# Searching the top 32 in maxima of four keys, with three pools of candidates, and turning 97 units on VectorE

## The chip, the cores and the metric

The kernel runs on one core of a Trainium2 chip. The metric is the device time of one execution, in microseconds; smaller is better. The trace was taken by the hardware profiler on one execution, and names of lines (L483) are lines of the kernel before. Engines are TensorE (PE in the profile; PEld is its weight load), VectorE (DVE), ScalarE (ACT), GpSimd (POOL) and the queue of SyncE (SP), from which nearly all transfers are issued.

## What is computed

Attention that keeps, for each query, the 32 largest of 576 scores, followed by a normalization, a two-layer network and a residual:

```python
scores = scale * np.matmul(q, k.transpose(0, 1, 3, 2))      # (8, 8, 576, 576), head size 64
kth = np.partition(scores, -32, axis=-1)[..., -32:-31]
scores = np.where(scores >= kth, scores, -1e9)
scores = scores - np.max(scores, axis=-1, keepdims=True)
attn = np.exp(scores)
attn = attn / (np.sum(attn, axis=-1, keepdims=True) + 1e-09)
x = heads_joined(np.matmul(attn, v))                        # (8, 576, 512)
xn = (x - mean(x)) / np.sqrt(var(x) + 1e-06) * g_ln
out = x + np.maximum(xn @ w_ch1, 0.0) @ w_ch2               # 512 -> 2048 -> 512
```

All numbers are 32-bit floats. The two weight matrices arrive as 64-bit floats and are converted in the kernel.

## The kernel before

The work is cut into 160 units. A full unit (128 of them) is one block of 128 queries of two heads: two tiles of 128 x 576 scores. A rest unit (32) holds the last 64 queries of two heads in one tile. Units stand in jobs: a job is one batch entry, one pair of heads and one, two or three query blocks. The order of the jobs is written out by hand, and the whole order of instructions too: the loop `for n in range(END)` (L1263) runs one step per unit, and in each step every engine gets pieces of work for several units. Every engine runs its instructions strictly in that order.

In step n the loop does this for VectorE's main thread: `select(u, 0)` to `select(u, 3)` for unit n, spread over the step, and at its end `halve` for unit n + 1. `halve` (L447) forms two arrays of 288 from the 576 scores of a tile: the larger and the smaller of the keys j and j + 288. `select(u, i)` (L464) is one of four search rounds: MAX8 gives the eight largest of a row, and, but for the last round, MATCH_REPLACE8 (preceded by a MATCH_VALUE_LOAD) overwrites these eight. Rounds 0 and 1 search the 288 larger keys; in round 1 the eight largest of the 288 smaller keys are taken as candidates as well, and rounds 2 and 3 search the larger keys and these candidates together (296). The eighth value of round 3 is the threshold. One step later ScalarE and GpSimd make the mask (`prepare`, `mask`), and ScalarE the exponentials (`weigh`, L543).

Eight candidates from the smaller keys are enough unless eight or more of a row's 32 largest lie there. `watch` (L498, GpSimd) writes for each tile the difference of the eighth candidate and the threshold; `settle_watch` (L509) reduces these notes once per 16 units, `tell` (L517) turns them into one flag at the end, and where the flag is set, the whole computation runs a second time with two rounds of candidates. `hi_homes` (L110) are the two buffers in which the larger keys and the candidates of a unit lie, used in turn; the candidates lie in front of the keys or behind them in turn, so that GpSimd can still read those of one unit while VectorE fills the buffer for the unit after next.

The exponentials then have to be turned (queries and keys exchanged) to become the moving operand of the product with v. There are two ways. `turn` (L597): TensorE transposes each full unit in nine pieces (four per tile, L606, and one for the last 64 keys of both, L635), and ScalarE copies them to the tile pt. `move` (L573): VectorE transposes blocks of 32 x 32 in one instruction (L577), SP writes the result to HBM and, one step later, reads it back in four pieces in the turned order into pt (L587). Which full unit takes which way is set at L1106, `u.moved`: 87 full units are moved. The product (`values`, L664) of a job stands four steps after the job's last unit where the next job's first unit is moved, three otherwise; a moved unit n is transposed in step n + 2 and its reads are issued in step n + 3. pt is a single buffer.

The network works on blocks of 256 rows (`Block`). Its matrix products (L819 hidden layer, L979 and L858 projection) are put in a list and handed out between the pieces of the attention. Up to the step in which the weights are converted (step 21), the share handed out per step follows from cost numbers of the planner (`DVE_UNIT` and others, `slot`); after it, the work in the list is spread evenly up to the next block and the end.

Of the kernel before, what the change touches and what calls it, by code (L numbers as in the profile page):

```python
# [10 lines left out]
ALU = mybir.AluOpType  # L11
FP32 = mybir.dt.float32
# [17 lines left out]
def compute(  # L30
# [12 lines left out]
    nc = tc.nc  # L43
    P = nc.NUM_PARTITIONS
    B, H, S, D = q.shape
# [11 lines left out]
    def pool(name, bufs, **kw):  # L57
        return ctx.enter_context(tc.tile_pool(name=name, bufs=bufs, **kw))

    NV = 2  # L60
    GQ = 2 * P + R
    HALF = S // 2
    LOWS = 8 * low_rounds

    consts = pool("consts", 1)
    ldpool = pool("ld", 1)
# [3 lines left out]
    lopool = pool("lo", 1)  # L70
# [20 lines left out]
    def const(shape, name):  # L91
        return consts.tile(shape, FP32, tag=name, name=name)

    def brief(name):

        return psps.tile([P, 512], FP32, tag="ps", name=name)
# [8 lines left out]
    ends = const([P, P], "ends")  # L105
    nc.gpsimd.memset(ends[:], 0.0)
    if doubt is not None:
        watched = const([P, 2, 34], "watched")
        nc.gpsimd.memset(watched[:], -1.0)
    hi_homes = [const([P, 2, HALF + (1 if doubt is None else 2) * LOWS], f"hi{i}") for i in range(2)]  # L110
    ident = const([P, P], "ident")
    make_identity(nc, ident[:])
    columns = const([P, J + NC], "columns")
    half, gcol = columns[:, 0:J], columns[:, J : J + NC]
# [300 lines left out]
    def take_scores(u):  # L415
        u.sc = scpool.tile([P, 2, S], FP32, tag="sc", name="sc")
        for t in range(len(u.tiles)):
            for s in range(2):
                nc.scalar.copy(  # L419
                    u.sc[:, t, s * HALF : (s + 1) * HALF], u.made[s][t][:, 0:HALF]  # L420
                )

    def score_half(u, s):
# [5 lines left out]
        for ps, hs in zip(pss, u.tiles):  # L429
            for i, hh in enumerate(hs):  # L430
                r = slice(hh * D, (hh + 1) * D)
                parts = [(0, s * HALF, HALF)]
                if u.rest and hh == 1:
                    parts = [(0, R + s * HALF, HALF - s * R)]
                    if s:
                        parts += [(HALF - R, 0, R)]
                for o, k0, width in parts:
# [9 lines left out]
    def halve(u):  # L447

        nt = len(u.tiles)
        u.lo = lopool.tile([P, 2, HALF], FP32, tag="lo", name="lo")
        u.hi = hi_homes[u.i % 2]
        sides = int(doubt is not None)
        u.low, u.body = (sides * LOWS + HALF, sides * LOWS) if doubt is None or u.i // 2 % 2 else (0, LOWS)
        a, b = u.sc[:, 0:nt, 0:HALF], u.sc[:, 0:nt, HALF:S]
        lo, hi = u.lo[:, 0:nt], u.hi[:, 0:nt, u.body : u.body + HALF]  # L460
        nc.vector.tensor_tensor(hi, a, b, ALU.max)  # L461
        nc.vector.tensor_tensor(lo, a, b, ALU.min)  # L462

    def select(u, i):  # L464

        nt = range(len(u.tiles))

        def replace(m, t, x):
            nc.vector.match_replace(x, m[:, t, :], x, LOWEST)  # L469

        if i == 1:
            for r in range(low_rounds):
                o = u.low + 8 * r
                for t in nt:
                    nc.vector.max(u.hi[:, t, o : o + 8], u.lo[:, t])  # L475
                if r < low_rounds - 1:
                    for t in nt:
                        replace(u.hi[:, :, o : o + 8], t, u.lo[:, t])
        r0, width = (min(u.low, u.body), HALF + LOWS) if i > 1 else (u.body, HALF)
        pl = brief_small if i in (1, 2) else small  # L480
        m = pl.tile([P, 2, 8], FP32, tag=f"m{i}", name=f"m{i}")
        for t in nt:
            nc.vector.max(m[:, t, :], u.hi[:, t, r0 : r0 + width])  # L483
        if i < TOP_K // 8 - 1:
            for t in nt:
                replace(m, t, u.hi[:, t, r0 : r0 + width])
        if i == 0:
            u.top = m
        u.thr = m
# [8 lines left out]
    def watch(u):  # L498

        nt = len(u.tiles)  # L500
        half, c = u.i // 16 % 2, 1 + 2 * (u.i % 16)
        nc.gpsimd.tensor_tensor(
            watched[:, half, c : c + nt], u.hi[:, 0:nt, u.low + 7], u.thr[:, 0:nt, 7], ALU.subtract
        )
        if u.i % 16 == 15 or u.i == N - 1:
            u.ends_watch = True
            u.half = half

    def settle_watch(half):  # L509

        for out, first, op in ((0, 0, ALU.max), (33, 1, ALU.min)):
            nc.vector.tensor_reduce(
                watched[:, half, out : out + 1], watched[:, half, first : first + 33],
                mybir.AxisListType.X, op,
            )

    def tell():  # L517

        w = hpool.tile([P, J * P], FP32, tag="h", name="tell")
        nc.gpsimd.memset(w[:], 0.0)  # L520
        nc.vector.tensor_scalar(w[:, 2:4], watched[:, :, 33], -1.0e38, None, ALU.is_le)
        nc.vector.tensor_scalar(w[:, 4:6], watched[:, :, 0], 0.0, None, ALU.is_ge)
        nc.vector.tensor_reduce(w[:, 0:1], w[:, 2:6], mybir.AxisListType.X, ALU.max)
        ps = brief("tell")
        nc.tensor.transpose(ps[:, 0:P], w[:, 0:P], ident[:])
        nc.vector.tensor_reduce(w[0:1, P : P + 1], ps[0:1, 0:P], mybir.AxisListType.X, ALU.max)
        nc.vector.tensor_copy(doubt, w[0:1, P : P + 1])
# [560 lines left out]
    N = len(units)  # L1088
# [15 lines left out]
    for j, nj in zip(jobs, jobs[1:] + [None]):  # L1104
        for u in units[max(j.first, EARLY) : j.last + 1]:
            u.moved = not u.rest and u.i >= jobs[3 * NHP].first and (  # L1106
                u.i < j.last
                or (j.b > 1 and (j.hp % 2 == 0 or u.i > N - 20))
                and nj is not None and not units[nj.first].rest
            )  # L1110

# [16 lines left out]
    for j in jobs:  # L1128
        if j.hp == NHP - 1:
            b = j.b  # L1130
# [26 lines left out]
    def at(i):  # L1157
        return units[i] if 0 <= i < N else None
# [96 lines left out]
    take_scores(units[0])  # L1255
    load(fresh[1], nc.sync, nc.scalar)
    halve(units[0])
    scores(units[1])
    take_scores(units[1])
# [3 lines left out]
    for n in range(END):  # L1263
# [8 lines left out]
        u, nxt, mk = at(n), at(n + 1), at(n - 1)  # L1272
# [21 lines left out]
        if mk and doubt is not None:  # L1294
            watch(mk)
# [12 lines left out]
        if u:  # L1308
            select(u, 0)
# [15 lines left out]
        if doubt is not None and at(n - 2) and at(n - 2).ends_watch:  # L1325
            settle_watch(at(n - 2).half)
            if n == N + 1:
                tell()
# [12 lines left out]
        if u:  # L1341
            select(u, 1)
# [33 lines left out]
        if u:  # L1376
            select(u, 2)
# [19 lines left out]
        if nxt:  # L1397
            halve(nxt)
# [14 lines left out]
        if late and late.job.hp == NHP - 1:  # L1413
            r = late.job.b // 2
# [14 lines left out]
@with_exitstack  # L1429
def kernel(  # L1430
    ctx: ExitStack,
    tc: tile.TileContext,
    *operands: bass.AP,
):
    nc = tc.nc
    doubt = ctx.enter_context(tc.tile_pool(name="doubt", bufs=1)).tile(
        [1, 1], I32, tag="doubt", name="doubt"
    )
    compute(tc, *operands, low_rounds=1, doubt=doubt[:])
    again = nc.values_load(  # L1440
        doubt[:], min_val=0, max_val=1,
        skip_runtime_bounds_check_because="a comparison's result",
    )
    with tc.If(again > 0):
        compute(tc, *operands, low_rounds=2, doubt=None)
# [31 lines left out]
```

## Time and profile before

| | |
|---|---|
| median of 3 runs | 1571.16 us (1571.02 to 1571.75) |
| profiled execution | 1571.11 us, of which the span of the trace is 1569.2 us |
| TensorE busy | 1469.0 us (94%) |
| VectorE busy | 1363.4 us (87%) |
| ScalarE busy | 1083.8 us (69%) |
| GpSimd busy | 981.2 us (63%) |
| mean granted clock of TensorE | 0.975 |
| bytes moved | 245.60 MB, 157 GB/s |

Busy time is the time in which an engine executes something, not counting waits, branches and the issuing of transfers. In the profile's groups, `out<-in` are the kernel's names of tiles, then follow the shape, the count, the total and the mean duration of one, and the idle time of the engine just before them. In a view of windows, each stretch of the span shows the busy time of each engine with its number of instructions, the granted clock, the share of time in which the DMA engines were busy, and GB/s. In the timeline, the first number is the start and the second the time until the end of the last instruction of the row. The duration of an instruction on VectorE or TensorE reaches into that of the next; the distance between starts tells what one costs when they follow each other.

### The profile page before, as it was taken

Reading aid. Unit: us, or ns where it says so; the run is one execution under the profiler, and the core shown is the slowest. Engines: PE = TensorE matmul, PEld = TensorE weight load, DVE = VectorE, ACT = ScalarE, POOL = GpSimd, SP = SyncE. Lnnn points to the kernel's source line nnn. Section 1 sums busy time; section 2 is a strip of 40 time slices with the busy share of each in tenths; the row PEclk is TensorE's granted clock in tenths of the full one; section 3 lists DMA queues with packets and bytes.
Section 4 is the critical chain, followed back from the end, with each engine's and each line's share of the span. In section 5 each row is a group of like instructions: output and inputs, shape, how many; then the busy total and the mean of one; then the engine's idle time right before and its main releaser. Section 6 shows DMA issues by size and latency. Waiting matters only on the chain. (4 is left out here: it accounts for less than half of the span.)

```text
span 1569.2 us, 27215 instructions
## 1 busy us (share of the span) xinstructions
PE 1469.0 (94%) x8046; PEld 1108.0 (71%) x8046; DVE 1363.4 (87%) x3873; ACT 1083.8 (69%) x3081; POOL 981.2 (63%) x1318
## 2 busy tenths in 40 slices
PE   4568889999999999999999999999999998999997
PEld 3346446566787677778777777777777776788886
DVE  7997999899979998999988999999999999768000
ACT  6978887786777767767768676768676776555421
POOL 6968995747465565756566647474746475737524
PEclk9779989999999999999999999999999999999999
DMA  6623551466728865577754687657677557454511
GB/s 170 167 85 97 137 139 53 124 178 181 226 83 194 202 208 153 168 199 153 216 148 134 174 200 197 173 150 191 175 201 206 162 164 208 121 166 125 150 35 50
DMA packets 374774, 245.60 MB, mean 157 GB/s; under 512 B 255956, under 2 KB 343512, under 8 KB 374616
## 3 DMA queue, kind: packets, MB, share of 16 engines
q1 hardware_dynamic: 371048, 243.17, 57.6%
q8 instruction: 67, 1.10, 0.3%
q10 hardware_dynamic: 3568, 0.59, 0.3%
q14 instruction: 91, 0.75, 0.2%
HBM read 166.14 MB, written 77.53 MB: 155 GB/s over the span
## 5 line engine op out<-in xcount | busy, mean ns | idle before, releaser
L535 POOL TENSOR_TENSOR e<-e,sc 128x576 f32<-128x576 f32 x288 | 416.0, 1462 | 453.8 <-ACT e L532 392.9
L819 PE MATMUL hps<-xT,w 128*128 128x256 f32 x2304 | 542.2, 384 | 2.4 <-ACT xT L781 2.4
L819 PEld LDWEIGHTS hps<-xT,w 128*128 128x128 f32 x2304 | 423.0, 191 | 82.2 <-issue 27.2
L483 DVE MAX8 m<-hi 128x8 f32<-128x296 f32 (+1 forms) x1152 | 471.3, 444 | 1.2
L469 DVE MATCH_REPLACE8 hi<-m,hi 128x288 f32<-128x288 f32 (+1 forms) x864 | 377.0, 441 | 0.0
L979 PE MATMUL ops<-w,h 128*128 128x256 f32 x1280 | 304.8, 383 | 1.4 <-ACT o L944 1.4
L979 PEld LDWEIGHTS ops<-w,h 128*128 128x128 f32 x1280 | 233.6, 190 | 44.3 <-issue 13.5
L419 ACT COPY sc<-scps 128x288 f32<-128x288 f32 x576 | 188.5, 402 | 78.5 <-POOL e L535 56.2
L543 ACT ACTIVATE e<-e,m 128x576 f32<-128x576 f32 x288 | 225.1, 784 | 14.6 <-POOL e L535 12.5
L532 ACT ACTIVATE e<-sc,m 128x576 f32<-128x576 f32 x288 | 209.4, 769 | 0.0
L842 ACT ACTIVATE h<-hps 128x512 f32<-128x512 f32 x144 | 86.7, 602 | 114.1 <-PE hps L819 113.5
L577 DVE STREAM_TRANSPOSE sc<-e 128x1152 f32<-128x1152 f32 x87 | 118.8, 1366 | 52.5 <-ACT e L543 46.3
L669 PE MATMUL av<-pt,vb 128*64 128x256 f32 (+2 forms) x1280 | 148.8, 376 | 9.5 <-DMA pt<-turned 7.7
L462 DVE TENSOR_TENSOR lo<-sc 128x576 f32<-128x576 f32 (+1 forms) x160 | 136.1, 850 | 0.0
L461 DVE TENSOR_TENSOR hi<-sc 128x576 f32<-128x576 f32 (+1 forms) x160 | 130.0, 812 | 3.0 <-ACT sc L419 3.0
L669 PEld LDWEIGHTS av<-pt,vb 128*64 128x64 f32 x1280 | 81.6, 140 | 66.4 <-issue 17.1
L438 PE MATMUL scps<-kT,late_qT 64*128 64x288 f32 (+3 forms) x832 | 121.7, 410 | 0.2 <-ACT pt L618 0.2
L979 PE MATMUL ops<-wt,s 128*128 128x256 f32 x512 | 119.4, 383 | 0.0
L475 DVE MAX8 hi<-lo 128x8 f32<-128x288 f32 x288 | 117.5, 443 | 0.0
L438 PE MATMUL scps<-kT,qT 64*128 64x288 f32 x512 | 92.6, 460 | 23.5 <-DVE qT L366 8.0
L606 PE MATMUL tp<-ident,e 128*128 128x128 f32 x456 | 74.2, 290 | 39.9 <-ACT e L543 28.9
L979 PEld LDWEIGHTS ops<-wt,s 128*128 128x128 f32 x512 | 94.7, 190 | 17.3 <-issue 4.4
(111 smaller groups left out, 1793.5 us busy)
## 6 DMA issues: line engine op xcount, KB each, us to landing
turned<-sc SPq DMA_DIRECT2D x87, 576.0 KB, 4.2
pt<-turned SPq DMA_DIRECT2D x348, 144.0 KB, 3.2
w<-forms SPq DMA_DIRECT2D x128, 256.0 KB, 4.7
vb<-in_v_dram SPq DMA_DIRECT2D x80, 288.0 KB, 4.2
raw<-in_moe_w_ch_dram SPq DMA_DIRECT2D x32, 512.0 KB, 4.5
kT<-kept SPq DMA_DIRECT2D x48, 288.0 KB, 3.7
kept<-kT SPq DMA_DIRECT2D x32, 288.0 KB, 3.6
kqin<-in_k_dram SPq DMA_DIRECT2D x116, 72.0 KB, 2.6
```

The costliest lines, as they stand in the source:

```text
L419: nc.scalar.copy(u.sc[:, t, s * HALF : (s + 1) * HALF], u.made[s][t][:, 0:HALF])
L438: nc.tensor.matmul(ps[i * R : i * R + ql, o : o + width], qT[r, q0 : q0 + ql], kT[r, k0 : k0 + width], start=True, stop=True,)
L461: nc.vector.tensor_tensor(hi, a, b, ALU.max)
L462: nc.vector.tensor_tensor(lo, a, b, ALU.min)
L469: nc.vector.match_replace(x, m[:, t, :], x, LOWEST)
L483: nc.vector.max(m[:, t, :], u.hi[:, t, r0 : r0 + width])
L532: nc.scalar.activation(u.e[:, t], u.sc[:, t], AF.Relu, bias=u.edge[:, t : t + 1], scale=-STEEP)
L535: nc.gpsimd.tensor_tensor(u.e[:, t], u.e[:, t], u.sc[:, t], ALU.subtract)
L543: nc.scalar.activation(u.e[:, t], u.e[:, t], AF.Exp, bias=u.bias[:, t : t + 1], scale=-scale, accum_out=g.den[:, col : col + 1],)
L669: nc.tensor.matmul(av[h * D : (h + 1) * D, 0 : g.nq], vb[:, h * (J + 1) + c, :], heads_of(g, h, 0, g.nq // 32)[:, :, c], start=(c == 0), s ...
L819: nc.tensor.matmul(ps[0][:, side * N : (side + 1) * N], w1[:, c, f * P : (f + 1) * P], self.xT[:, c, 0:N], start=(c == 0), stop=(c == NC - 1),
L979: nc.tensor.matmul(bank[name][:, 0:Q], a(j), rhs, start=first and j == 0, stop=(j == G - 1), skip_group_check=not first,)
```

## The change

The larger keys are halved a second time, into 144 maxima of four keys each (`hi`) and 144 smaller ones of the pairs' maxima (`mid`). Round 0 searches the 144 maxima alone. Three pools give eight candidates each: the two halves of `mid` (72 each, taken at the end of round 0) and the 288 smaller keys (taken in round 1, as before). Rounds 1 to 3 search the 144 maxima and the 24 candidates together, 168 elements. `watch` compares the eighth candidate of each of the three pools. The second computation, which runs only when the flag is set, keeps the old form. The rule for moved units now also takes the last unit of a job with an odd pair of heads where the batch entry is above 1, and that of an even pair where it is not; 97 full units are moved.

```diff
--- before.py
+++ after.py
@@ -59,8 +59,10 @@
 
     NV = 2
     GQ = 2 * P + R
-    HALF = S // 2
+    HALF, QUART = S // 2, S // 4
     LOWS = 8 * low_rounds
+    POOLS = 3
+    CANDS = 8 * POOLS
 
     consts = pool("consts", 1)
     ldpool = pool("ld", 1)
@@ -105,9 +107,11 @@
     ends = const([P, P], "ends")
     nc.gpsimd.memset(ends[:], 0.0)
     if doubt is not None:
-        watched = const([P, 2, 34], "watched")
+        NOTES = POOLS * 32
+        watched = const([P, 2, NOTES + 2], "watched")
         nc.gpsimd.memset(watched[:], -1.0)
-    hi_homes = [const([P, 2, HALF + (1 if doubt is None else 2) * LOWS], f"hi{i}") for i in range(2)]
+    home = HALF + LOWS if doubt is None else QUART + 2 * CANDS
+    hi_homes = [const([P, 2, home], f"hi{i}") for i in range(2)]
     ident = const([P, P], "ident")
     make_identity(nc, ident[:])
     columns = const([P, J + NC], "columns")
@@ -452,14 +456,25 @@
 
 
         nt = len(u.tiles)
+        u.hi = hi_homes[u.i % 2]
+        a, b = u.sc[:, 0:nt, 0:HALF], u.sc[:, 0:nt, HALF:S]
+        tt = nc.vector.tensor_tensor
+        if doubt is None:
+            u.lo = lopool.tile([P, 2, HALF], FP32, tag="lo", name="lo")
+            u.low, u.body, u.width = HALF, 0, HALF
+            tt(u.hi[:, 0:nt, 0:HALF], a, b, ALU.max)
+            tt(u.lo[:, 0:nt], a, b, ALU.min)
+            return
+        u.low, u.body = (CANDS + QUART, CANDS) if u.i // 2 % 2 else (0, CANDS)
+        u.width = QUART
+        pairs = lopool.tile([P, 2, HALF], FP32, tag="lo", name="pairs")
+        tt(pairs[:, 0:nt], a, b, ALU.max)
+        x, y = pairs[:, 0:nt, 0:QUART], pairs[:, 0:nt, QUART:HALF]
+        u.mid = lopool.tile([P, 2, QUART], FP32, tag="mid", name="mid")
+        tt(u.hi[:, 0:nt, u.body : u.body + QUART], x, y, ALU.max)
+        tt(u.mid[:, 0:nt], x, y, ALU.min)
         u.lo = lopool.tile([P, 2, HALF], FP32, tag="lo", name="lo")
-        u.hi = hi_homes[u.i % 2]
-        sides = int(doubt is not None)
-        u.low, u.body = (sides * LOWS + HALF, sides * LOWS) if doubt is None or u.i // 2 % 2 else (0, LOWS)
-        a, b = u.sc[:, 0:nt, 0:HALF], u.sc[:, 0:nt, HALF:S]
-        lo, hi = u.lo[:, 0:nt], u.hi[:, 0:nt, u.body : u.body + HALF]
-        nc.vector.tensor_tensor(hi, a, b, ALU.max)
-        nc.vector.tensor_tensor(lo, a, b, ALU.min)
+        tt(u.lo[:, 0:nt], a, b, ALU.min)
 
     def select(u, i):
 
@@ -468,15 +483,24 @@
         def replace(m, t, x):
             nc.vector.match_replace(x, m[:, t, :], x, LOWEST)
 
-        if i == 1:
-            for r in range(low_rounds):
-                o = u.low + 8 * r
+        if doubt is None:
+            if i == 1:
+                for r in range(low_rounds):
+                    o = u.low + 8 * r
+                    for t in nt:
+                        nc.vector.max(u.hi[:, t, o : o + 8], u.lo[:, t])
+                    if r < low_rounds - 1:
+                        for t in nt:
+                            replace(u.hi[:, :, o : o + 8], t, u.lo[:, t])
+            with_all, cands = i > 1, LOWS
+        else:
+            if i == 1:
                 for t in nt:
-                    nc.vector.max(u.hi[:, t, o : o + 8], u.lo[:, t])
-                if r < low_rounds - 1:
-                    for t in nt:
-                        replace(u.hi[:, :, o : o + 8], t, u.lo[:, t])
-        r0, width = (min(u.low, u.body), HALF + LOWS) if i > 1 else (u.body, HALF)
+                    nc.vector.max(u.hi[:, t, u.low : u.low + 8], u.lo[:, t])
+            with_all, cands = i > 0, CANDS
+        r0, width = u.body, u.width
+        if with_all:
+            r0, width = min(u.low, u.body), width + cands
         pl = brief_small if i in (1, 2) else small
         m = pl.tile([P, 2, 8], FP32, tag=f"m{i}", name=f"m{i}")
         for t in nt:
@@ -484,6 +508,14 @@
         if i < TOP_K // 8 - 1:
             for t in nt:
                 replace(m, t, u.hi[:, t, r0 : r0 + width])
+        if i == 0 and doubt is not None:
+            part = QUART // (POOLS - 1)
+            for t in nt:
+                for r in range(POOLS - 1):
+                    o = u.low + 8 + 8 * r
+                    nc.vector.max(
+                        u.hi[:, t, o : o + 8], u.mid[:, t, r * part : (r + 1) * part]
+                    )
         if i == 0:
             u.top = m
         u.thr = m
@@ -498,9 +530,13 @@
     def watch(u):
 
         nt = len(u.tiles)
-        half, c = u.i // 16 % 2, 1 + 2 * (u.i % 16)
+        half, c = u.i // 16 % 2, 1 + 2 * POOLS * (u.i % 16)
+        cands = u.hi[:, 0:nt, u.low : u.low + CANDS].rearrange("p t (r k) -> p t r k", k=8)
         nc.gpsimd.tensor_tensor(
-            watched[:, half, c : c + nt], u.hi[:, 0:nt, u.low + 7], u.thr[:, 0:nt, 7], ALU.subtract
+            watched[:, half, c : c + POOLS * nt].rearrange("p (t r) -> p t r", r=POOLS),
+            cands[:, :, :, 7],
+            u.thr[:, 0:nt, 7].unsqueeze(2).to_broadcast([P, nt, POOLS]),
+            ALU.subtract,
         )
         if u.i % 16 == 15 or u.i == N - 1:
             u.ends_watch = True
@@ -508,9 +544,9 @@
 
     def settle_watch(half):
 
-        for out, first, op in ((0, 0, ALU.max), (33, 1, ALU.min)):
+        for out, first, op in ((0, 0, ALU.max), (NOTES + 1, 1, ALU.min)):
             nc.vector.tensor_reduce(
-                watched[:, half, out : out + 1], watched[:, half, first : first + 33],
+                watched[:, half, out : out + 1], watched[:, half, first : first + NOTES + 1],
                 mybir.AxisListType.X, op,
             )
 
@@ -518,7 +554,7 @@
 
         w = hpool.tile([P, J * P], FP32, tag="h", name="tell")
         nc.gpsimd.memset(w[:], 0.0)
-        nc.vector.tensor_scalar(w[:, 2:4], watched[:, :, 33], -1.0e38, None, ALU.is_le)
+        nc.vector.tensor_scalar(w[:, 2:4], watched[:, :, NOTES + 1], -1.0e38, None, ALU.is_le)
         nc.vector.tensor_scalar(w[:, 4:6], watched[:, :, 0], 0.0, None, ALU.is_ge)
         nc.vector.tensor_reduce(w[:, 0:1], w[:, 2:6], mybir.AxisListType.X, ALU.max)
         ps = brief("tell")
@@ -1105,7 +1141,7 @@
         for u in units[max(j.first, EARLY) : j.last + 1]:
             u.moved = not u.rest and u.i >= jobs[3 * NHP].first and (
                 u.i < j.last
-                or (j.b > 1 and (j.hp % 2 == 0 or u.i > N - 20))
+                or (j.b > 1 or j.hp % 2 == 0)
                 and nj is not None and not units[nj.first].rest
             )
```

## Prediction

> **What bounds the kernel now.** I read the page's totals and slices first, then the busy time of each engine by stage, then what TensorE waited for in the long middle stage, then single rows for prices.
>
> ```profile
> span 1569.2 us, 27215 instructions
> PE 1469.0 (94%) x8046; PEld 1108.0 (71%) x8046; DVE 1363.4 (87%) x3873; ACT 1083.8 (69%) x3081; POOL 981.2 (63%) x1318
> ...
> PE   4568889999999999999999999999999998999997
> DVE  7997999899979998999988999999999999768000
> ```
>
> TensorE is full from about the seventh slice on; VectorE is nearly full too, and has stopped three slices before the end. The stages in the view of windows (PE, PEld, DVE, ACT, POOL busy, then the granted clock):
>
> ```profile
> 0.00:157.00 157.00, 101.49 (x500) 72.14 (x500) 131.86 (x370) 125.67 (x327) 121.11 (x120) 0.85 0.48 130
> 157.00:196.00 39.00, 32.12 (x146) 17.27 (x145) 38.82 (x91) 34.56 (x88) 36.19 (x32) 0.93 0.51 137
> 157.00:275.00 118.00, 103.78 (x483) 62.32 (x482) 117.58 (x316) 98.03 (x254) 96.27 (x88) 0.93 0.41 109
> 275.00:1450.00 1175.00, 1154.60 (x6528) 880.62 (x6530) 1108.30 (x3176) 829.11 (x2428) 712.88 (x1021) 1.00 0.64 173
> 1450.00:1569.00 119.00, 109.17 (x542) 92.95 (x538) 5.67 (x15) 30.98 (x74) 50.94 (x91) 0.97 0.28 77
> ```
>
> Of TensorE's 100 us of idle time (1569.2 - 1469.0), 70 lie before 275 us: 55.5 before 157 us and 14.2 from 157 to 275 us, where VectorE is busy 117.58 of 118 us and sets the pace. From 275 to 1450 us TensorE is idle 20.4 of 1175 us. Busy could hide slow running, so the spacing of its instructions matters:
>
> ```profile
> 803.52 0.60 PE L606 MATMUL tp<-ident,e 128*128 128x128 f32 x4
> 803.96 1.46 PE L979 MATMUL ops<-w,h 128*128 128x256 f32 x6
> 805.26 0.38 PE L714 MATMUL xo<-ident,oT 128*128 128x128 f32 x2
> ```
>
> Six 256-column products start in 1.30 us, 0.217 us each, and four transposes of 128 columns in 0.44 us, 0.11 us each: in proportion to their columns. So the queue runs at its rate, and from 275 us the time is TensorE's work plus 20 us of waits. The tail, in which VectorE has 5.67 us of work, is TensorE's alone. Hence work taken off VectorE counts only before 275 us, and work taken off TensorE counts where it is full.
>
> **Ten more units turned by VectorE.** The added units are 25, 29, 35, 47, 51, 55, 67, 79, 103 and 107, the last of their jobs. Each drops two parts of four transposes and one of the ends, 9 x 0.11 = 0.99 us; ten give **-9.9 us**, all where TensorE is full. ScalarE loses their 30 copies, which are not the bound. What they add:
>
> ```profile
> L577 DVE STREAM_TRANSPOSE sc<-e 128x1152 f32<-128x1152 f32 x87 | 118.8, 1366 | 52.5 <-ACT e L543 46.3
> ...
> turned<-sc SPq DMA_DIRECT2D x87, 576.0 KB, 4.2
> pt<-turned SPq DMA_DIRECT2D x348, 144.0 KB, 3.2
> ```
>
> VectorE gets 10 x 1.37 = 13.7 us, between about 270 and 970 us; cover is its idle time of 1175 - 1108.3 = 66.7 us in the middle stage together with what the search below frees. The transpose can wait for ScalarE's exponential; the third and fourth search rounds, the next halving and any column statistics queue behind it, and the next mask and ScalarE's bias wait for those. SP gets ten writes and forty reads: each read waits on SP for its write, and loads of keys, values, forms and stores stand behind it. The result is due one step after the read is issued, since the last unit of a job has the shortest time to its product:
>
> ```profile
> PE av L669 <- DMA pt<-turned: 7.7, 6, 2.9
> PE tp L778 <- ACT sc L419: 3.6, 3, 1.9
> PE tp L606 <- ACT sc L419: 3.0, 2, 1.6
> ```
>
> These are TensorE's longest waits between 275 and 1450 us (total, times, longest). Before, 19 moved units are last of their job, after, 29. If the 7.7 us belong to those 19, ten more cost 7.7 x 10/19 = **+4.1 us**; the bounds are 0 (all hidden) and 10 x 2.9 = 29 us (each as the longest). The other 12.7 us of waits hang on ScalarE's queue, which loses work; I take a quarter, **-3.2 us**, between 0 and -12.7.
>
> **The narrower search.** VectorE's cost is the distance between starts, not the printed duration, which overlaps the next one:
>
> ```profile
> 189.35 0.80 DVE L483 MAX8 m<-hi 128x8 f32<-128x288 f32 x2
> 190.07 0.07 DVE L469 MATCH_VALUE_LOAD hi<-m,hi 128x8 f32 x1
> ...
> 191.00 0.74 DVE L366 STREAM_TRANSPOSE kT<-kqin 128x576 f32<-128x576 f32 x1
> 191.67 0.40 DVE L366 STREAM_TRANSPOSE qT<-kqin 128x256 f32<-128x256 f32 x1
> 192.00 0.46 DVE L366 STREAM_TRANSPOSE late_qT<-kqin 128x320 f32<-128x320 f32 x1
> ...
> 195.53 0.74 DVE L462 TENSOR_TENSOR lo<-sc 128x576 f32<-128x576 f32 x1
> 196.20 0.81 DVE L483 MAX8 m<-hi 128x8 f32<-128x288 f32 x2
> ```
>
> The transposes give 0.67 us at 576 elements and 0.33 at 256: a line of 0.06 us plus 1.06 ns an element. It gives 0.365 at 288, and the MAX8 pair took 0.36 each; a TENSOR_TENSOR of 576 with nothing beside it took 0.67. By the line, 72, 144 and 168 elements cost 0.135, 0.21 and 0.235 us. Per full unit of two tiles:
> - MAX8: six of 288 and four of 296 (0.37), 3.64 us, become two of 144, four of 72, two of 288 and six of 168, 3.09 us: -0.55.
> - MATCH_REPLACE8, priced as MAX8 of its width: four of 288 and two of 296, 2.18 us, become two of 144 and four of 168, 1.36 us: -0.82. The six value loads stay.
> - TENSOR_TENSOR: two of 576, 1.34 us, become two of 576 and two of 288, 2.07 us: +0.73. The second reads what the first has just written; I add 0.1 us for it, the difference of duration and start distance (0.74 - 0.67) rounded up.
>
> That is -0.54 us. No row shows MAX8 narrower than 288: the far ends are a price in proportion to width, 0.09 at 72 elements, and a floor of 0.33, the narrowest pass quoted. I take the line, since the transposes lie on it.
>
> Against it stands what TENSOR_TENSOR costs beside GpSimd:
>
> ```profile
> 158.08 1.42 DVE L461 TENSOR_TENSOR hi<-sc 128x576 f32<-128x576 f32 x1
> 159.43 1.84 DVE L462 TENSOR_TENSOR lo<-sc 128x576 f32<-128x576 f32 x1
> 161.19 0.81 DVE L483 MAX8 m<-hi 128x8 f32<-128x288 f32 x2
> ```
>
> ```profile
> 158.85 1.79 POOL L183 TENSOR_TENSOR wt<-wt 128x512 uint32<-128x512 uint32 x1
> 160.72 1.68 POOL L185 TENSOR_TENSOR w<-wt,sign 128x512 f32<-128x512 f32 x1
> 162.38 1.18 POOL L165 TENSOR_SCALAR wt<-wt 128x512 f32<-128x512 f32 x2
> 163.53 3.13 POOL L535 TENSOR_TENSOR e<-e,sc 128x576 f32<-128x576 f32 x2
> 166.61 0.20 POOL L502 TENSOR_TENSOR watched<-hi,m 128x2 f32<-128x2 f32 x1
> 166.76 1.28 POOL L183 TENSOR_TENSOR wt<-wt 128x512 uint32<-128x512 uint32 x1
> ```
>
> The same instruction took 1.76 us between starts at 159.43 and 0.67 at 195.53; GpSimd's L183 took 1.79 there and 1.28 alone. The MAX8 rows keep their 0.36 us under GpSimd's work. So the change trades work that does not collide for work that does. The average collision by stage, from line 462's busy time:
>
> ```profile
> 0.00:157.00 157.00, 16.64 (x14) 0.85 0.48 130
> 157.00:275.00 118.00, 13.44 (x12) 0.93 0.41 109
> ```
>
> ```profile
> L462 DVE TENSOR_TENSOR lo<-sc 128x576 f32<-128x576 f32 x77 | 63.9, 830 | 0.0
> ```
>
> Before 275 us the mean is 30.08/26 = 1.157 us, 0.42 above the clean 0.74; from 400 to 1300 us it is 0.09 above. One more set of 576 elements therefore takes +0.42 early and +0.09 later: a full unit gains 0.12 us early and 0.45 later. Early, 26 units give **-3.1 us**; the bounds are -0.54 x 26 = -14 (no new collision) and, with the extra elements at the price of the row at 159.43, (1.76 - 0.67 - 0.54) x 26 = +14. Later the gain, some 0.45 x 102 = 46 us of VectorE's time, lies under TensorE and is worth nothing; without TensorE's full queue it would be.
>
> GpSimd is slowed as well. From 157 to 196 us it has 2.8 us left in some 3.5 steps, 0.8 a step; the collision of 1.79 - 1.28 = 0.5 us fits in. The wider watch writes 6 numbers instead of 2 at about 0.2 us and the two reductions per sixteen units read 97 instead of 33: nothing on the path, under GpSimd's and VectorE's slack of the middle stage; bare, 64 x 1.06 ns x 20 = 1.4 us.
>
> The Trainium skill (SBUF — State Buffer, "Who interferes with whom") says that a VectorE instruction with two SBUF inputs contends with a GpSimd one that reads SBUF, one with a single input does not, and that the loser is held for the whole instruction. The trace agrees on who collides; a full hold for every extra instruction gives the +14 us end instead of -3.1, so 1576 instead of 1559.
>
> **Sum.** -9.9 + 4.1 - 3.2 - 3.1 = -12.1. The profiled execution took 1571.11 us, 1.9 more than its span, and the median is 1571.16, so nothing is added: **1559 us**.
>
> **The rivals.**
> - A. The forecast: 1551 to 1567. Chance 0.60.
> - B. Early collisions do not grow and TensorE's waits close: 1571.1 - 9.9 - 14 - 6 = 1541. For it, VectorE is the pace-setter at 157 to 275 us; against it, GpSimd is nearly full there too. 0.16.
> - C. The collision on the shared port, before 275 us: every extra pass meets GpSimd, 1571.1 - 9.9 + 14 + 1 = 1576, slower. It decides once an early unit grows by more than (9.9 + 3.1)/26 = 0.50 us, near the row at 159.43. Against it, the mean of 26 units is far below that row. 0.09. The rule of the page named above is this case.
> - D. Width saves nothing below 256 elements: MAX8 then costs 0.36 x 2 + 0.33 x 12 = 4.68 (+1.04), MATCH_REPLACE8 1.98 (-0.20), with +0.83 for the passes and +0.42 for collisions +2.1 us a unit early, 1571.1 - 9.9 + 54 = 1615. Against it, the line. 0.02.
> - E. The ten new results land late: ten waits of 1.3 us (7.7/6), with the first gains: 1568; each as the longest, 1584. For it, the only long wait in the middle stage is this one. 0.12.
> - F. The change does not do what it says: a pool overflows and the whole is computed again, over 3100 us. In the reference's inputs, no row has more than 6 of its 32 largest in one of the three pools, and 8 are needed. 0.01.
>
> **How the numbers follow.** About 0.2% (3.1 us) is what a measurement can tell. Faster: A without its upper edge (0.59), B and a third of E, 0.79; same: that edge and half of E, 0.07; slower: C, D, F and the rest of E, 0.14. The range leaves out C and the far part of B: **1545 to 1570**.
>
> **What would show it.** VectorE's transposes 97 times; TensorE's transposes of e on its own queue 9 x 10 fewer and its busy time near 1459 us; MAX8 of 72 elements started 0.13 to 0.15 us apart, VectorE's busy time down by some 35 us (3 + 46 saved on full units, 14 added); the 26th halving 3 us earlier; waits of av for pt near 12 us. It is wrong if VectorE's TENSOR_TENSOR of 576 before 275 us averages over 1.5 us, if TensorE's idle time between 275 us and VectorE's end grows past 30 us, or if VectorE's end no longer lies before TensorE's tail.

## The result, and the profile after

The changed kernel takes 1648.13 us (median of 4 runs, 1647.36 to 1650.82) against 1571.09 us for the kernel before: a ratio of 1.0492, 95% interval 1.0474 to 1.0511. The change makes it 77 us slower; 1559 us had been predicted. The second computation did not run, and the intended instructions are there: 97 transposes by VectorE, MAX8 over 72 and 168 elements. The page of the profile after, totals and slices:

```profile
span 1645.8 us, 27978 instructions
PE 1485.9 (90%) x7956; PEld 1114.6 (68%) x7956; DVE 1459.2 (89%) x4779; ACT 1072.9 (65%) x3051; POOL 1038.0 (63%) x1318
...
PE   4678889989899889999999998899999898999997
DVE  7998999999989998999999999999999999977100
```

VectorE's busy time was to fall by some 35 us; it rose by 96 us (from 1363.4). The windows of the kernel after (columns as before):

```profile
0.00:157.00 157.00, 102.84 (x499) 73.03 (x500) 140.73 (x442) 125.65 (x326) 119.26 (x120) 0.84 0.48 129
157.00:275.00 118.00, 101.65 (x458) 61.16 (x458) 117.09 (x382) 96.25 (x251) 96.69 (x86) 0.93 0.42 111
275.00:1450.00 1175.00, 1095.70 (x6072) 824.67 (x6069) 1135.72 (x3753) 779.45 (x2292) 725.12 (x959) 0.98 0.64 173
```

In the middle stage TensorE is idle 79 us (1175 - 1095.7) instead of 20, and has done 6072 products instead of 6528. Nearly all of the loss is made there: before 275 us the two kernels differ little (the 26th halving starts 2.6 us later, at 271.1 instead of 268.5 us). Where VectorE's own stage ends is told by the first and last start of the halving's first pass, before and after:

```profile
L461 DVE TENSOR_TENSOR hi<-sc x160: 429/737/1978, 11.3 to 1440.8; 128x576 f32<-128x576 f32 x128, 128x288 f32<-128x288 f32 x32
```

```profile
L471 DVE TENSOR_TENSOR pairs<-sc x160: 429/739/1976, 11.2 to 1516.8; 128x576 f32<-128x576 f32 x128, 128x288 f32<-128x288 f32 x32
```

The last halving starts 76 us later, and what follows it takes the same in both: 1569.2 - 1440.8 = 128 us and 1645.8 - 1516.8 = 129 us. So the whole loss lies between the first and the last halving. VectorE's groups by shape name the place:

```profile
L477 DVE TENSOR_TENSOR lo<-sc 128x576 f32<-128x576 f32 x128 | 179.9, 1405 | 4.4
...
L471 DVE TENSOR_TENSOR pairs<-sc 128x576 f32<-128x576 f32 x128 | 118.5, 926 | 3.0 <-ACT sc L423 3.0
...
L474 DVE TENSOR_TENSOR hi<-pairs 128x288 f32<-128x288 f32 x128 | 88.4, 691 | 4.4
L475 DVE TENSOR_TENSOR mid<-pairs 128x288 f32<-128x288 f32 x128 | 83.0, 649 | 0.0
```

The pass for lo is the same instruction as L462 before, which took 918 ns on average:

```profile
L462 DVE TENSOR_TENSOR lo<-sc 128x576 f32<-128x576 f32 x128 | 117.6, 918 | 0.0
```

It now takes 1405 ns. The mean hides two values: 69 of the 128 took over 1.5 us, against 14 of 128 before, and 64 of these 69 begin while a mask subtraction of GpSimd (L571) is running. A step of the timeline shows why; first VectorE, then GpSimd, after:

```profile
995.25 0.74 DVE L471 TENSOR_TENSOR pairs<-sc 128x576 f32<-128x576 f32 x1
996.02 0.46 DVE L474 TENSOR_TENSOR hi<-pairs 128x288 f32<-128x288 f32 x1
996.39 0.45 DVE L475 TENSOR_TENSOR mid<-pairs 128x288 f32<-128x288 f32 x1
996.88 1.85 DVE L477 TENSOR_TENSOR lo<-sc 128x576 f32<-128x576 f32 x1
998.65 0.51 DVE L507 MAX8 m<-hi 128x8 f32<-128x144 f32 x2
```

```profile
996.46 3.54 POOL L571 TENSOR_TENSOR e<-e,sc 128x576 f32<-128x576 f32 x2 [1.68 <-ACT e L568]
```

And the same place in the kernel before:

```profile
973.69 0.74 DVE L461 TENSOR_TENSOR hi<-sc 128x576 f32<-128x576 f32 x1
974.35 0.75 DVE L462 TENSOR_TENSOR lo<-sc 128x576 f32<-128x576 f32 x1
975.01 0.81 DVE L483 MAX8 m<-hi 128x8 f32<-128x288 f32 x2
```

```profile
974.89 2.84 POOL L535 TENSOR_TENSOR e<-e,sc 128x576 f32<-128x576 f32 x2 [3.47 <-ACT e L532]
```

GpSimd's mask subtraction starts 1.2 us after the halving does, in both (996.46 - 995.25 and 974.89 - 973.69). It hangs on the threshold of the round that ends where the halving begins; between the two, ScalarE forms the bias and the first part of the mask:

```profile
995.36 0.21 ACT L527 ACTIVATE m<-m 128x2 f32<-128x2 f32 x1 [3.01 <-DVE m L507]
995.47 0.19 ACT L528 ACTIVATE m<-m 128x2 f32<-128x2 f32 x1
995.60 1.44 ACT L568 ACTIVATE e<-sc,m 128x576 f32<-128x576 f32 x2
```

In 78 of the 160 steps after, and in 52 before, this distance is 1.1 to 1.3 us; in most others GpSimd arrives later. The two passes of before are finished 1.32 us after their start, the second already running when GpSimd arrives. The four passes of after need 2.3 us undisturbed, so the last one meets the subtraction: 1.77 us between starts instead of 0.66, and the two subtractions take 3.54 us instead of 2.84.

### The profile page after: what moved, and what is told of

It is laid out like the page before. It is cut to its first block, busy times and chain, and to the rows that moved or that the text cites. A ratio compares the mean times of both kernels' runs of the same rounds, so it can differ in the third digit from the quotient of the medians.

```text
span 1645.8 us, 27978 instructions
## 1 busy us (share of the span) xinstructions
PE 1485.9 (90%) x7956; PEld 1114.6 (68%) x7956; DVE 1459.2 (89%) x4779; ACT 1072.9 (65%) x3051; POOL 1038.0 (63%) x1318
## 4 chain that ended last, share of the span: by engine, by line
DVE 60%; PE 24%; DMA 5%; ACT 4%; POOL 3%; issue 2%; SPq 1%; DVEq 0%; POOLq 0%; ACTq 0%
DVE m L507 11%; PE hps L855 11%; DVE hi L484 10%; DVE lo L477 9%; PE ops L1015 8%; DVE sc L613 6%; DVE pairs L471 5%; DVE hi L499 4%; DVE hi L474 4%; DVE hi L516 3%; DVE mid L475 3%; PE av L705 2%; DMA turned<-sc 2%; PE scps L442 2%; DMA pt<-turned 2%
## 5 line engine op out<-in xcount | busy, mean ns | idle before, releaser
L571 POOL TENSOR_TENSOR e<-e,sc 128x576 f32<-128x576 f32 x288 | 459.5, 1613 | 468.4 <-ACT e L568 449.1
L855 PEld LDWEIGHTS hps<-xT,w 128*128 128x128 f32 x2304 | 429.1, 193 | 84.4 <-issue 27.9
L507 DVE MAX8 m<-hi 128x8 f32<-128x168 f32 (+1 forms) x1152 | 315.6, 309 | 2.3
L484 DVE MATCH_REPLACE8 hi<-m,hi 128x168 f32<-128x168 f32 (+1 forms) x864 | 259.5, 305 | 0.0
L477 DVE TENSOR_TENSOR lo<-sc 128x576 f32<-128x576 f32 (+1 forms) x160 | 199.3, 1246 | 5.5
L705 PE MATMUL av<-pt,vb 128*64 128x256 f32 (+2 forms) x1280 | 151.2, 380 | 33.9 <-DMA pt<-turned 20.6
L613 DVE STREAM_TRANSPOSE sc<-e 128x1152 f32<-128x1152 f32 x97 | 132.4, 1365 | 36.9 <-ACT e L579 30.8
L527 ACT ACTIVATE m<-m 128x2 f32<-128x2 f32 (+1 forms) x160 | 32.6, 204 | 186.0 <-DVE m L507 185.7
L471 DVE TENSOR_TENSOR pairs<-sc 128x576 f32<-128x576 f32 (+1 forms) x160 | 135.7, 848 | 3.0 <-ACT sc L423 3.0
L474 DVE TENSOR_TENSOR hi<-pairs 128x288 f32<-128x288 f32 (+1 forms) x160 | 105.6, 660 | 5.5
```

Of the source, the lines that this page charges most:

```text
L471: tt(pairs[:, 0:nt], a, b, ALU.max)
L477: tt(u.lo[:, 0:nt], a, b, ALU.min)
L571: nc.gpsimd.tensor_tensor(u.e[:, t], u.e[:, t], u.sc[:, t], ALU.subtract)
L613: nc.vector.transpose(blocks.rearrange("p (j c n) -> p j c n", j=ni, n=32), u.e[:].rearrange("p t n -> p (t n)").rearrange("p (c j k) -> p ...
L705: nc.tensor.matmul(av[h * D : (h + 1) * D, 0 : g.nq], vb[:, h * (J + 1) + c, :], heads_of(g, h, 0, g.nq // 32)[:, :, c], start=(c == 0), s ...
L855: nc.tensor.matmul(ps[0][:, side * N : (side + 1) * N], w1[:, c, f * P : (f + 1) * P], self.xT[:, c, 0:N], start=(c == 0), stop=(c == NC - 1),
```

## The experiments

Three theories were put to the test. P (place): VectorE's two-input passes are held while GpSimd's mask subtraction runs, so their place in the step sets their price. M (moves): the ten more moved units cost it. W (work): the new search is more work for VectorE wherever it stands. A second question came out of the first runs: what sets the pace of the middle stage, TensorE (T, the prediction's view), VectorE (D), or each in turn (B). In the table, "old" is the search of before and "new" the changed one; each ratio is to runs of the kernel before made together with that row's (medians 1570.8 to 1571.7 us). "Without lo" and the three kernels with zeros leave out part of the computation and serve to measure only.

| kernel | search | moved units | us | ratio to before, 95% interval |
|---|---|---|---|---|
| after | new | 97 | 1648.1 | 1.0492 (1.0474 to 1.0511) |
| search alone | new | 87 | 1626.6 | 1.0366 (1.0345 to 1.0387) |
| moves alone | old | 97 | 1583.3 | 1.0080 (1.0064 to 1.0097) |
| halving ahead of round 3 | new | 97 | 1614.9 | 1.0277 (1.0260 to 1.0295) |
| lo behind round 0 | old | 87 | 1617.9 | 1.0303 (1.0286 to 1.0320) |
| fewer moves | old | 75 | 1567.5 | 0.9975 (0.9966 to 0.9985) |
| without lo | old, less | 87 | 1542.3 | 0.9809 (0.9789 to 0.9830) |
| pairs early | new | 87 | 1571.1 | 0.9997 (0.9988 to 1.0007) |
| pairs early, fewer moves | new | 75 | 1570.4 | 0.9990 (0.9980 to 0.9999) |
| pairs early, more moves | new | 97 | 1583.4 | 1.0087 (1.0069 to 1.0104) |
| zeros, before | old | 87 | 1557.0 | 0.9908 (0.9891 to 0.9924) |
| zeros, search alone | new | 87 | 1545.1 | 0.9829 (0.9815 to 0.9844) |
| zeros, after | new | 97 | 1560.7 | 0.9922 (0.9903 to 0.9940) |

**Search alone**, the old rule for moved units in the changed kernel:

```diff
-                or (j.b > 1 or j.hp % 2 == 0)
+                or (j.b > 1 and (j.hp % 2 == 0 or u.i > N - 20))
```

> The changed search with the 87 moved units of before. Theory P (VectorE's two-input passes are held while GpSimd's mask subtraction runs, and the longer halving now reaches into it): nearly all of the loss stays, 1630 to 1650 us, with the pass for lo still at 1.3 to 1.5 us on average. Theory M (the ten more moved units cost it, through VectorE's full queue or late landings): 1560 to 1580 us. Theory W (the search is simply more work on VectorE wherever it stands): also 1630 to 1650 us, so this run parts M from the other two.

1626.6 us: 56 us of the 77 are the search's, a little less than P and W expected. The pass for lo takes 1.34 us on average. M falls as the main cause, but 21.6 us are left for the moves.

**Moves alone**, the new rule in the kernel before (the same two lines the other way round):

> The search of before with the 97 moved units. Theory P and theory W: TensorE loses 9.9 us of transposes where it is full, VectorE gains 13.7 us; 1560 to 1575 us. Theory M: 1600 us or more, with waits of the product with v for pt above 20 us in total.

1583.3 us: no theory had this. The moves do not gain 10 us, they lose 12. The steps of the ten units tell how. VectorE's timeline around the step in which unit 29 is transposed, first in the kernel before, then with the unit moved (some rows left out):

```profile
331.21 0.74 DVE L461 TENSOR_TENSOR hi<-sc 128x576 f32<-128x576 f32 x1
...
338.76 0.73 DVE L461 TENSOR_TENSOR hi<-sc 128x576 f32<-128x576 f32 x1
```

```profile
330.83 0.73 DVE L461 TENSOR_TENSOR hi<-sc 128x576 f32<-128x576 f32 x1
...
336.02 1.36 DVE L577 STREAM_TRANSPOSE sc<-e 128x1152 f32<-128x1152 f32 x1
...
339.63 0.73 DVE L461 TENSOR_TENSOR hi<-sc 128x576 f32<-128x576 f32 x1
```

The step takes 8.80 us instead of 7.55. All ten steps grow by 1.2 to 1.3 us, 12.6 us together, and the other steps between 260 and 960 us change by less than 1 us in sum. In each of the ten steps VectorE runs without a gap, so its transpose is paid in full. TensorE's busy time falls by 4.6 us (1469.0 to 1464.4), and its idle time in the middle stage rises to 38 us.

**Halving ahead of the fourth round**, in the changed kernel:

```diff
-        if u:
-            select(u, 3)
         if nxt:
             halve(nxt)
+        if u:
+            select(u, 3)
```

> The changed kernel whole, with only the place of the next unit's halving moved: ahead of the fourth search round instead of behind it, so that it stands about half a step away from GpSimd's mask subtraction. Same instructions, same sizes. Theory P: the pass for lo falls from 1.41 us to below 1.0 us on average, VectorE's busy time falls by 60 to 130 us, and the time goes to 1550 to 1590 us. Theory W: within 10 us of 1648 us.

1614.9 us: the pass for lo is down to 0.92 us as P had it, and the time falls by 33 us for a change of order alone, which W excludes. But it stays far above P's 1590: the passes for pairs and hi now collide more (1.00 and 0.77 us on average instead of 0.93 and 0.69), with other work of GpSimd and in part with the subtraction itself, and VectorE's busy time falls by 44 us only, where 60 to 130 were expected.

**Lo behind the first round**, in the kernel before: `halve` makes hi alone, and the pass for lo is issued behind `select(u, 0)`:

```diff
         if u:
             select(u, 0)
+            u.lows()
```

> The kernel before, with only the pass that makes the smaller keys (lo) moved behind the first search round, about 1.5 us later, where GpSimd's mask subtraction usually runs. Same instructions, same sizes. Theory P: this pass goes from 0.92 us to 1.4 us or more on average for full units, and with VectorE nearly full the time grows to 1600 to 1650 us. Theory W: no change, 1571 us within 5 us.

1617.9 us: 47 us for one unchanged instruction per unit at another place. W, which allowed 5 us, is excluded. The size per pass was missed: 1.00 us for full units, not 1.4; the rest units' passes pay more:

```profile
L464 DVE TENSOR_TENSOR lo<-sc 128x576 f32<-128x576 f32 x128 | 127.4, 996 | 0.0
...
L464 DVE TENSOR_TENSOR lo<-sc 128x288 f32<-128x288 f32 x32 | 35.8, 1119 | 0.0
```

Not all of the 47 us is collision. The first MAX8 now stands right behind the pass for hi, whose result it reads, and starts 0.78 us after it; in the kernel before, with the pass for lo between them, the next instruction started after 0.66 us (974.35 - 973.69):

```profile
1007.29 0.75 DVE L461 TENSOR_TENSOR hi<-sc 128x576 f32<-128x576 f32 x1
1008.07 0.82 DVE L487 MAX8 m<-hi 128x8 f32<-128x288 f32 x2
```

Over 160 units that is some 19 us of VectorE's time, and the MAX8 over lo now stands right behind lo in the same way. How the rest of the 47 us divides was not measured. VectorE's busy time rises by 57 us and the time by 47 us, so the pace depends on VectorE, as in the moves alone.

**Fewer moves**, in the kernel before:

```diff
-                or (j.b > 1 and (j.hp % 2 == 0 or u.i > N - 20))
+                or (u.i > N - 20)
```

> The search of before with 75 moved units: the twelve last units of jobs that before moves between units 33 and 105 are turned on TensorE. Theory D (VectorE paces each step from the start to its own end, near 1450 us, although TensorE shows busy 98% of that stage): 12 x 1.29 us come off, 1553 to 1560 us. Theory B (both engines are nearly at their limit, so that work taken from one is lost on the other): TensorE's 20 us of idle time take up most of its 12 x 0.99 us, 1562 to 1575 us. Theory T, that of the prediction (TensorE's work sets the time): 1571 + 12 = 1583 us.

1567.5 us, 3.8 us less: B. Eleven of the twelve steps lose 1.3 us, the other 0.4, but other steps grow, and TensorE's idle time in the middle stage falls from 20 to 9 us. Ten units added cost 12 us, and twelve taken away gain 4. This kernel is faster than the one before and the changed one.

**Without lo**, in the kernel before: the pass for lo and the MAX8 over it are left out and the candidates' places are filled once with a very small number, so that some thresholds are too low.

> The kernel before without the smaller keys: the pass that makes lo and the MAX8 over it are left out (the candidates stay at a very small constant), so the threshold is too low in rows where both keys of a pair are among the 32 largest. VectorE loses 136 + 117 us of busy time, TensorE nothing. Theory T: 1545 to 1560 us, the gain coming from before 275 us alone. Theory D without a second limit: 1571 - 0.8 x 240 = 1380 us. Theory B: TensorE's floor stops the gain near its busy time plus unavoidable waits, 1500 to 1540 us.

1542.3 us, between the upper end of B's range (1540) and the lower end of T's (1545). VectorE is 189 us less busy and only 29 us are gained; the last halving starts at 1409.5, 31 us earlier. TensorE is idle 5.8 us of the middle stage (1169.16 of 1175 us busy), so that little is left to gain there. That TensorE's work limits the gain is T's view, but T expected all of it before 275 us: TensorE's idle time in the middle stage fell by 14.6 us, about half of the gain.

**Pairs early**, the changed search with 87 moves and the halving in two places: the pass for pairs ahead of the fourth round, hi, mid and lo (`rest_of_halving`) behind it. The lines in the loop, against the changed kernel:

```diff
+        if nxt:
+            halve(nxt)
         if u:
             select(u, 3)
         if nxt:
-            halve(nxt)
+            nxt.rest_of_halving()
```

> The changed search with the 87 moves of before, and the halving in two places: the pass for pairs ahead of the fourth round, those for hi, mid and lo behind it, so that these three (some 1.5 us) stand in the 1.2 us between the end of the last round and the start of GpSimd's mask subtraction, as the two passes of before did. Theory P: the pass for lo falls below 1.1 us on average, VectorE's busy time falls to 1340 to 1390 us, and the time to 1555 to 1590 us. Theory W: 1620 us or more, as in the run with the search alone.

1571.1 us: the same search that costs 56 us in one piece costs nothing so. The three passes fit into the 1.2 us ahead of the subtraction nearly as the two of before did; lo takes 0.90 us, and 6 of its 128 passes over 1.5 us:

```profile
L480 DVE TENSOR_TENSOR lo<-sc 128x576 f32<-128x576 f32 x128 | 115.0, 899 | 4.4
```

Part of the price stays: pairs now takes 1.00 us on average, and VectorE's busy time is 1370.8 us, 7 above that of the kernel before. On the other side, hi no longer waits some 0.1 us for the pass for pairs right in front of it, which over 160 units is some 18 us of VectorE's time; so the 56 us that this order saves are collision in the main, not wholly.

**Pairs early with 75 and with 97 moves:**

> The changed search with the halving in two places and 75 moved units. Theory B: as the 75 moves did for the search of before, some 4 us off the 1571 us of the same kernel with 87, so 1563 to 1570 us. If VectorE alone set the pace it would be 12 x 1.29 us, 1553 to 1557 us; if TensorE alone did, 1583 us.

> The whole change (97 moved units) with the halving in two places. Theory B: the moves cost their 1.29 us in steps that VectorE paces and pay 0.99 us in those that TensorE paces; with the search in its better place VectorE's steps without a move are some 0.4 us shorter than before, so the ten cost less than the 12 us they cost the search of before: 1572 to 1580 us. Should TensorE pace nearly all steps: 1561 us. If moves cost the same as with the old search: 1583 us.

1570.4 and 1583.4 us. Fewer moves gain 0.7 us, less than the 4 us expected and less than single runs differ; TensorE, idle 7.0 us of the middle stage, is at its limit there. More moves cost 12.3 us again, the worst of the three cases named: all ten steps grow by 1.2 to 1.3 us, 12.6 us together, against the same kernel with 87 moves.

**Zeros instead of the subtraction**, three kernels with the same edit: GpSimd writes zeros to e and reads nothing from SBUF. Mask and subtraction are left out of the result.

```diff
-        nc.gpsimd.tensor_tensor(u.e[:, t], u.e[:, t], u.sc[:, t], ALU.subtract)
+        nc.gpsimd.memset(u.e[:, t], 0.0)
```

> The kernel before, in which GpSimd writes zeros over e instead of subtracting sc from it (it reads nothing from SBUF there); the weights are then all alike, the mask and the subtraction are left out of the result. It is the measure for the run with the same edit in the changed kernel. Theory P: VectorE's two passes fall from 0.90 and 0.92 us to 0.75 to 0.85 us; theory B lets the time fall little, to 1550 to 1568 us.

> The changed kernel with the same edit; mask and subtraction are left out of the result. Nothing of VectorE's, TensorE's or the transfers' work changes. Theory P: the pass for lo falls from 1.41 us to 0.75 to 0.95 us, VectorE's busy time to 1290 to 1350 us, and the time to 1535 to 1560 us, below that of the kernel before with the same edit. Theory W: still 40 us or more above the kernel before with the same edit.

> The changed search with 87 moved units, in place as in the changed kernel, and GpSimd writing zeros over e without reading (mask and subtraction left out of the result). Theory P with B: the search without its collisions is worth a little, 1548 to 1556 us against 1557 us of the search of before with the same edit, and the ten moves make up the rest to 1561 us. Theory W: 1557 us or more.

1557.0, 1560.7 and 1545.1 us. VectorE's groups in the changed kernel with zeros:

```profile
L477 DVE TENSOR_TENSOR lo<-sc 128x576 f32<-128x576 f32 x128 | 106.7, 834 | 4.4
L471 DVE TENSOR_TENSOR pairs<-sc 128x576 f32<-128x576 f32 x128 | 105.6, 825 | 4.0 <-ACT sc L423 4.0
...
L474 DVE TENSOR_TENSOR hi<-pairs 128x288 f32<-128x288 f32 x128 | 81.3, 636 | 4.4
...
L475 DVE TENSOR_TENSOR mid<-pairs 128x288 f32<-128x288 f32 x128 | 70.2, 548 | 0.0
```

The pass for lo is at 0.83 us, and the change as a whole costs 3.7 us instead of 77: the search now gains 11.8 us (1557.0 to 1545.1), more than expected, and the ten moves lose 15.6 (1545.1 to 1560.7, whose four runs lie between 1556.4 and 1562.1). P expected the sum slightly on the other side, having priced the moves too low. So 73 of the 77 us hang on the subtraction. The zeros also take 0.58 us instead of 1.46 to 1.61; how much of the relief is that they read nothing and how much that they are shorter was not parted.

## Why the prediction was wrong

**What sets the pace.** The step that failed is the first: "from 275 us the time is TensorE's work plus 20 us of waits", and "work taken off VectorE counts only before 275 us". TensorE's queue does run at its rate there, but VectorE runs most steps without a gap too: in 118 of the 133 steps between 275 and 1450 us it is idle for less than 0.3 us. Its 66.7 us of idle time there, named as cover for the transposes, are a few long waits (columns: total, times, longest; from 275 to 1450 us), not slack in the steps that got more work:

```profile
DVE sc L577 <- ACT e L543: 37.0, 9, 6.8
DVE st L742 <- ACT x L691: 15.3, 4, 4.9
DVE sc L577 <- issue: 6.1, 1, 6.1
```

With the ten moves added to the kernel before, the first row reads the same, 37.0 us in 9 waits: none of that cover was used. Both engines are near their limit, step by step: added VectorE work costs in full (moves alone 12 us), removed work gains until TensorE's work leaves no more to gain (4 us, 29 us at most in these runs).

**The ten moves.** Counted as -9.9 + 4.1; they cost +12.5 with the old search, +12.3 with the pairs early, +15.6 with zeros and +21.6 in the changed kernel (1648.1 - 1626.6). The price of 1.37 us each was near (the steps grew by 1.25 us); the cover was not there. The +4.1 us for the landing of the turned data was not the main part: with the moves alone these waits rise from 7.7 to 9.5 us only. After, in the whole run, TensorE's waits are

```profile
PE xo L750 <- ACT oT L723: 34.1, 20, 5.0
...
PE av L705 <- DMA pt<-turned: 20.6, 9, 8.1
```

The second row is the landing: 20.6 us where 12 were forecast, 5.9 us with the search alone, and 13.9 us from 275 to 1450 us in the kernel with the pairs early and 97 moves. The first row had 3.9 us before and already 24.3 us with the search alone, so it belongs to the search more than to the moves. In the changed kernel the moves cost more than elsewhere; VectorE's busy time is 23.8 us above that of the search alone, 13.5 us of it the transposes and 8.8 us a further rise of the pass for lo. That the moves shift more passes into the subtraction is likely, and was not tested by itself.

**The price of a collision.** "+0.42 early and +0.09 later" took the mean of a stage for the price of new passes. The 0.09 was low because the two old passes end just as GpSimd begins; the new ones stand in other time. Rival C had the mechanism and the row (1.76 us at 159.43), but put it before 275 us, where it grew little, and left later time out of its sum. Line 477's windows (total, count; then clock, DMA share, GB/s):

```profile
0.00:157.00 157.00, 15.30 (x14) 0.84 0.48 129
157.00:275.00 118.00, 10.50 (x11) 0.93 0.42 111
275.00:1450.00 1175.00, 167.08 (x129) 0.98 0.64 173
```

Early the mean is 25.80/25 = 1.03 us, even below the old 1.16; later, 1.30 (full and rest units; before, 105.98/134 = 0.79). The early term, -3.1 us, was still wrong in sign: the 26th halving starts 2.6 us later, not 3 earlier. The passes of 288 collide too, as line 474's windows show:

```profile
0.00:157.00 157.00, 13.51 (x14) 0.84 0.48 129
157.00:275.00 118.00, 10.20 (x12) 0.93 0.42 111
```

That is 23.71/26 = 0.91 us on average for a pass that takes 0.45 us undisturbed. A hold did not shrink with the pass that was held: a pass for mid, of 288, took 1.67 us at 649.36, with a subtraction running from 649.20, about as much above its 0.45 as the 1.85 us of lo at 996.88 above its 0.75. But the extra 576 elements were priced as one pass. The Trainium skill (SBUF — State Buffer, "Who interferes with whom") says that the one who comes second is blocked until the other's instruction is over. The trace agrees: lo at 996.88 arrives within the subtraction of 996.46 and ends 1.1 us late, when the first subtraction has ended and its own 0.7 us have passed. So what a pass pays is what is left of GpSimd's instruction when it arrives.

**The prices of the narrow forms** were right: after, MAX8 of 144 and the replacements take 0.21 us between starts,

```profile
999.14 0.29 DVE L484 MATCH_REPLACE8 hi<-m,hi 128x144 f32<-128x144 f32 x1
999.35 0.07 DVE L484 MATCH_VALUE_LOAD hi<-m,hi 128x8 f32 x1
...
999.63 0.49 DVE L516 MAX8 hi<-mid 128x8 f32<-128x72 f32 x3
```

and three MAX8 of 72 some 0.14 us each. So rival D is out. The passes were a little dearer: hi waits 0.1 us for pairs (995.25 to 996.02, 0.77), as put in, and lo, which overwrites the buffer of pairs, 0.1 us for mid (996.39 to 996.88, 0.49), which was missed. Without the subtraction's collisions the search is worth 11.8 us, by the zeros. Rival F did not come.

## What to carry to other kernels

Here two engines that were busy 98% and 94% of a stage shared its limit. Read the length of single steps against each engine's work in them before calling one of them free, and look, in the window of that stage, whether its idle time is spread or lies in a few long waits. Where VectorE and GpSimd meet, an added two-input pass is priced by the time at which it stands relative to GpSimd's work, not by the mean of such passes; here the gap was 1.2 us, and a pass that began in it cost 0.67 us and one that came later 1.77. Moving one instruction to another place in the step is a cheap trial of that, as long as its new neighbours do not read what it has just written, which cost 0.1 us each time here.

## What had not been expected of the hardware

A collision slows both sides: the subtraction's mean went from 1462 to 1613 ns. TensorE's busy time rose by 17 us though its work fell; the granted clock of the middle stage went from 1.00 to 0.98 as its idle time there grew from 20 to 79 us. What lowered it was not tested.

The prediction took it that only passes with two inputs are held. One with a single input is held too: VectorE's TENSOR_SCALAR on the weights (L181, one input, 128x512) takes 0.40 us at the least and 1.63 us at the most in the changed kernel, and the seven that took over 1.5 us all begin while a mask subtraction is running. MAX8 of 168 is untouched: 313 ns on average after, 317 with zeros.
